# Two-product values at every fourth tile, and a transform family at both ends of one tile

## Chip, cores and metric

The kernel runs on one core of a Trainium2 chip. The metric is the time on the device in microseconds, as the median of several executions. The core has the engines TensorE (PE in the profile; its weight loads are PEld), VectorE (DVE), ScalarE (ACT), GpSimd (POOL) and SyncE (SP), which work side by side and wait for each other through semaphores.

## The reference

```python
X = np.fft.fft(x, axis=1)            # x: 8 x 3008 x 256, float32
X = np.fft.fft(X, axis=2)
y = X.real.reshape(24064, 256)
gate = np.maximum(y @ w_gate, 0.0)   # w_gate, w_val: 256 x 1536
val = y @ w_val
out = gate * val @ w_out             # w_out: 1536 x 256
```

## The kernel before, in words

**Transform.** The transform along the channels is worked into the weights (WA for cosines, WB for sines, WM = -2 WB). The one along the sequence is done by products with tables of cosines and sines, one batch ahead of its use. Its input is folded by symmetry on GpSimd first (`fold_steps`), spread over the tiles by a budget of microseconds per tile (`fold_us`, `run_fold`). The result of a batch is a cosine part U and a sine part V. A batch needs four families of six products (L589): three for one half (`par` 1), copied from PSUM to `es` by ScalarE (L598, `turned_out`), then three for the other half added in the same bank, copied by ScalarE (L601) and combined with `es` by two operations on VectorE (L603, `sums`). From batch 1 on both halves use the one bank d.

**Tiles.** From batch 1 on each batch has three thirds of columns (512, 512 and 481) and in each third 12 tiles of 128 hidden units, so 36 tiles, here numbered 0 to 35. A tile gives 2n columns of the hidden array `h`, since U and V give a value at a row and at its mirror image: the gate and the value are each taken for cosine plus sine and for cosine minus sine.

**A normal tile** ("n") has five products on TensorE:
- L1021 (`sine_part`, bank g) and L1028 (`cosine_part`, bank p). ScalarE puts a bias row into p beforehand (`seed`, L1016) and copies g (L1024). VectorE combines them to the one gate sum (`both`, L1032), GpSimd to the other (L1033).
- L876 and L877 (`value`, bank v): the value at the row. VectorE multiplies it with the rectified gate into the first half of `h` (`relu_mult(.., 0)`, L912).
- L882 (`mirror`): adds to v to make the value at the mirror row, one tile later. VectorE then writes the second half of `h` (`second`, L912 again).

**A two-product tile** (`st["short"]`) has no L882. Its value is built in bank d, of which there is one: ScalarE puts a bias row there two tiles ahead (`seed_value`, L1049), L1053 adds the cosine product one tile ahead (`value_cosine`), ScalarE copies the double of it (L1054), and L1058 adds the sine product (`value_sine`, weights WV, which L1247 makes in batch 2). The mirror value is the doubled copy less bank d. In batches 2 to 5 VectorE subtracts it into bank d itself (L1065, `own`), and `second` is on VectorE; in batches 6 and 7 it subtracts into the copy (L1067) and GpSimd multiplies (L1068). Before, these are tiles 14, 20, 26 and 32 in batches 2 to 5, 14, 18, 22, 26, 30 and 34 in batch 6, and nine in batch 7.

**A joined tile** ("j") makes up for the extra operation on VectorE: its sine product (L1043) is added to p one tile later, ScalarE makes both copies (L1039, L1044), GpSimd subtracts (L1045), and it has no L1032. Before, these are tiles 17, 23, 29 and 35 in batches 2 to 5, three behind each two-product tile.

**The order.** `slot` issues one tile's work for four tiles at once: `cur` (value, first half), `mid` (one ahead: L1043, L1053), `nxt` (two ahead: sine, cosine, `both`) and `pending` (one back: mirror, second half). All engines execute their own instructions in the order of this program. Between the products of a tile stand output products of the third before (L784, 12 per 128 rows, two such groups to a bank o; an eviction by ScalarE, L797, then DMAs by SyncE, L809): `outs` of them per slot, 8 or 7 by `per_tile`, plus or minus some by tile. `out(5)` has issued five eighths of them by the time of L1028; the rest stands at the slot's end. `outs` loses two in the slot ahead of a two-product tile, gains one in its own and in the one behind it, gains two where `nxt` is joined and loses two where `mid` is. `DFT_EVEN` says how many of a batch's 24 transform products follow each slot.

Of the kernel before, what the change touches and what calls it, by code (L numbers as in the profile page):

```python
# [15 lines left out]
ALU = mybir.AluOpType  # L16
# [18 lines left out]
def kernel(  # L35
# [808 lines left out]

    DFT_0 = (0, 0, 0, 0, 0, 3, 0, 0, 4, 3, 3, 0), (0, 0, 0, 0, 0) + (1,) * 7, (3, 3, 3, 3, 3, 3, 0, 0, 0, 0, 0, 0)

    DFT_EVEN = (3, 3, 0) * 4 + (0,) * 24
    DFT_1 = (3, 0, 3, 0, 0, 0) * 4 + (0, 1, 0, 1, 1) + (0,) * 7
    todo_out, todo_dft, todo_fold = [], [], []
    credit, paired = 0, False  # L850
# [2 lines left out]
    def run(todo, n):  # L853
        for _ in range(min(n, len(todo))):
            todo.pop(0)()
        if not paired:
            flush()

    def run_one(todo):
        if todo:  # L860
            todo.pop(0)()
# [53 lines left out]
    def second(st):  # L915
        (relu_mult if "s" in st else mult)(st, 1)
        if st["n"] == 481:
            keep_rest(st)
# [77 lines left out]
    SHORT = (2, 6, 10)  # L996

    def new_tiles():
        for b in range(1, B):
            for blk, block in enumerate(thirds):  # L1000
                for fi in range(NF):
                    st = tile_of(block, fi, uv[b])
                    st["b"] = b
                    mixed = 1 < b < 6 and blk > 0
                    st["kind"] = "o" if (b, blk, fi) == (1, 0, 6) else "j" if mixed and fi in (5, 11) else "n"
                    st["own"] = mixed
                    st["short"] = mixed and fi in (2, 8) or (b, blk) in ((6, 1), (6, 2), (7, 0), (7, 1)) and fi in SHORT or (b, blk) == (7, 2) and fi in (2, 5, 8)
                    st["lead"] = (b, blk, fi) == (1, 0, 0)
                    yield st

# [49 lines left out]
    def value_second(st):  # L1060
        n = st["n"]
        a = st["a"][:, 0:n]
        if st["own"]:
            v = st["v"][:, 0:n]
            nc.vector.tensor_tensor(v, a, v, op=ALU.subtract)  # L1065
            return
        nc.vector.tensor_tensor(a, a, st["v"][:, 0:n], op=ALU.subtract)  # L1067
        nc.gpsimd.tensor_tensor(half_h(st, 1), st["s"][2][:, 0:n], a, op=ALU.mult)  # L1068
        if n == 481:
            keep_rest(st)  # L1070

    def slot(cur, mid, nxt, after, outs, fold_us):

        joined, ready = (st is not None and st["kind"] == "j" for st in (nxt, mid))
        outs += 2 * joined - 2 * ready
        outs += cur["short"] + (pending is not None and pending.get("short", False)) - 2 * (mid is not None and mid["short"])
        stop = len(todo_out)

        def out(part):
            run(todo_out, len(todo_out) - stop + outs * part // 8)  # L1080
        old = nxt is not None and nxt["kind"] == "o"
        new = nxt is not None and nxt["kind"] == "n"
        early = cur["b"] > 1
        if early:
            run_one(turned_out)
            run_one(sums)
            if not todo_dft:
                run_one(sums)
        if old:
            gate(nxt)  # L1090
        lead = cur["lead"]
        out(4 if lead else 0)
        if new and mid["kind"] != "o":
            sine_part(nxt)
        out(4 if lead or nxt is None else 5)
        if new and mid["kind"] == "o":
            sine_part(nxt)
        if ready:
            add_sine(mid)
        if (new or joined) and not lead:  # L1100
            cosine_part(nxt)
        if joined:
            copy_cosine(nxt)
        if not lead:
            seed(after)
        if pending is not None and pending.get("short"):
            value_second(pending)
        elif pending is not None:
            mirror(pending["v"], pending, 1)
            second(pending)  # L1110
        if cur["short"]:
            value_sine(cur)
        else:
            value(cur)
        if mid is not None and mid["short"]:
            value_cosine(mid)
        if cur["kind"] == "o":
            mult(cur, 0, cur["first"])
        else:
            relu_mult(cur, 0)  # L1120
        if pending is not None and pending.get("short") and pending["own"]:
            second(pending)
        if lead:
            out(5)
            cosine_part(nxt)
            seed(after)
        if new:
            both(nxt)
        if old:
            nxt["first"] = nxt["r"]  # L1130
            mirror(nxt["g"], nxt, 0)
            relu(nxt)
        if cur["short"] and not cur["own"]:
            sm = cur["s"][2][:, 0:cur["n"]]
            nc.scalar.activation(sm, sm, ACTF.Relu)
        if nxt is not None and nxt["short"]:
            seed_value(nxt)
        run_fold(fold_us)
        if turned_out and not early:
            run_one(turned_out)  # L1140
        elif not joined:
            run_one(evict)
        if not early:
            run_one(sums)
        out(8)
        return cur
# [4 lines left out]
    for b in range(B):  # L1151
# [4 lines left out]
        for blk, block in enumerate(blocks):  # L1156
# [44 lines left out]
            if (b, blk) == (0, 0):  # L1201
                for fi in range(NF):
                    st = tile_of(block, fi, (U, V, CB))
                    add_h(st, hs)
                    if fi == 8:
                        todo_out = out_steps(b, block, hs, True)
                    pending = first_tile(st, more.get((0, fi), ()), 6)
                mirror(pending["g"], pending, 0)
                relu(pending)
            elif not paired:  # L1210
                for fi in range(NF):
                    st = tile_of(block, fi, (U, V, CB))
                    add_h(st, hs)
                    tag = {(3, 8): "g", (3, 9): "d", (3, 10): "g", (3, 11): "d"}.get((blk, fi), "p")
                    last = []
                    if (blk, fi) == (3, 11):
                        last = [lambda: (sine_part(ahead[1]), cosine_part(ahead[1]), both(ahead[1]), seed(ahead[2]))]
                    if (blk, fi) == (3, 9):
                        ahead = [next(tiles) for _ in range(3)]
                        more[(3, 9)] += [lambda: seed(ahead[0])]  # L1220
                        more[(3, 10)] += [lambda: seed(ahead[1])]
                        more[(3, 11)] += [lambda: (sine_part(ahead[0]), cosine_part(ahead[0]), both(ahead[0]))]
                    if (blk, fi) == (1, 8):
                        run(todo_out, len(todo_out))
                        todo_out = out_steps(b, block, hs, True)
                    st["widen"] = (blk, fi) in ((3, 6), (3, 7))
                    pending = single_tile(st, 3 if blk == 1 else per_tile // 2, more_b.get((blk, fi), ()), last, tag)
                    run(todo_dft, DFT_0[blk - 1][fi])
            else:
                for fi in range(NF):  # L1230
                    at = NF * blk + fi
                    cur = ahead.pop(0)
                    add_h(cur, hs)
                    ahead.append(next(tiles, None))
                    if b < 2:
                        outs = per_tile + ((-2, 0, -2, 2, 2, 0)[fi % 6] if per_tile == 7 else 0)
                    else:
                        outs = per_tile + (0 if blk or b == B - 1 else (-1, -1, 2)[fi % 3])
                    if (b, blk) == (B - 1, 2) and fi > 8:
                        outs = (10, 9, 19)[fi - 9]  # L1240
                        if fi == 9:
                            rest = out_steps(b, block, hs)
                            early, rest = rest[:10] + rest[12:16], rest[10:12] + rest[16:]
                            todo_out += early
                    if (b, at) in ((2, 5), (2, 9), (2, 13)):
                        f = slice(128 * (at - 5), 128 * (at - 1))
                        nc.scalar.mul(WV[:, f], WM[1][:, f], -0.5)  # L1247
                    if (b, at) == (2, 0):
                        nc.sync.dma_start(out=WB[0][0:1, :], in_=WM[0][0:1, :])
                    pending = slot(cur, *ahead, outs, .72 if b < 2 else (.76, .54, .54)[blk])  # L1250
                    for step in more_1.get(at, ()) if b == 1 else ():
                        step()
                    run(todo_dft, DFT_1[at] if b == 1 else DFT_EVEN[at])
            if b or blk > 1:
                run(todo_out, len(todo_out))
            if blk == len(blocks) - 1 or (b, blk) == (0, 1):
# [41 lines left out]
```

## Time and profile before

| | |
|---|---|
| median of 3 runs | 621.99 us (621.98 to 622.07) |
| the profiled execution | 621.7 us, of it 619.6 us span |
| granted TensorE clock | 1.00 |
| instructions with a busy time | 4032 on TensorE, 978 on VectorE, 911 on ScalarE, 493 on GpSimd |

The span reaches from the first to the last instruction that the trace has. A row of the timeline has the start, the duration, the engine, the line, the operation, what it writes and reads, and its size; "x2" means two merged in one row, and a bracket at its end the idle time of that engine before it and what ended it. A row of the groups has the count, the busy time, the mean duration in ns of one, and the idle time before them. Matmuls overlap: their durations are latencies, and what a product costs the engine is the distance from its start to the next.

### The profile page before, as it was taken

To read this page: it belongs to the slowest core of one execution; us is meant where nothing else is said; L and a number is where in the kernel's file an instruction comes from. 1 tells how busy PE (TensorE), PEld (TensorE's weight loads), DVE (VectorE), ACT (ScalarE), POOL (GpSimd) and SP (SyncE) were. 2 spreads that over 40 slices of the span, in tenths; PEclk is the share of its full clock that TensorE was granted. 3 is DMA by queue.
4 is the path that set the end of the run, shared out by engine and by line. 5 is a ranking of instruction groups with operands and counts; after the bars stand their busy time and mean duration, and the time that the engine had idled before them with its cause. 6 is when DMAs were issued, how large, how long until landed. Compare 5 with 4: busy or idle time off the path is not lost.

```text
span 619.6 us, 12415 instructions
## 1 busy us (share of the span) xinstructions
PE 610.7 (99%) x4032; PEld 395.3 (64%) x4076; DVE 549.5 (89%) x978; ACT 485.4 (78%) x911; POOL 520.5 (84%) x493
## 2 busy tenths in 40 slices
PE   8999999999999999999999999999999999999997
PEld 2566666666666666666666666666666666666666
DVE  8886677999899999899999999989999999999991
ACT  7796667776778888778887788777887799999982
POOL 8988992898999989899888988898896588888880
PEclk9999999999999999999999999999999999999999
DMA  9965758735263515524164321621111111211113
GB/s 242 214 199 133 169 175 113 185 75 153 76 152 138 168 52 110 177 76 152 37 159 154 114 94 42 143 70 60 53 44 55 60 44 39 60 52 53 48 47 105
DMA packets 86035, 66.48 MB, mean 107 GB/s; under 512 B 41639, under 2 KB 69063, under 8 KB 85970
## 3 DMA queue, kind: packets, MB, share of 16 engines
q1 hardware_dynamic: 81384, 60.02, 35.5%
q0 software_dynamic: 3984, 4.92, 4.0%
q8 instruction: 32, 0.52, 0.4%
q10 hardware_dynamic: 602, 0.75, 0.3%
q14 instruction: 33, 0.27, 0.2%
HBM read 41.89 MB, written 34.17 MB: 123 GB/s over the span
## 4 chain that ended last, share of the span: by engine, by line
PE 95%; DVE 1%; POOL 1%; issue 1%; DMA 1%; ACT 0%; DVEq 0%; POOLq 0%; ACTq 0%
PE o L784 39%; PE v L877 10%; PE v L882 9%; PE p L1028 8%; PE g L1021 8%; PE v L876 7%; PE d L589 4%; PE p L882 1%; PE d L1058 1%; PE d L1053 1%; PE p L876 1%; PE p L877 1%; DMA XG<-in_x_dram,gidx 1%; PE o L427 1%; PE p L1043 1%
## 5 line engine op out<-in xcount | busy, mean ns | idle before, releaser
L1033 POOL TENSOR_TENSOR r<-r 128x512 f32<-128x512 f32 (+1 forms) x235 | 293.4, 1254 | 75.0 <-DVE r L1032 73.8
L784 PE MATMUL o<-wo,h 128*128 128x256 bf16 x2172 | 328.6, 272 | 0.0
L912 DVE SCALAR_TENSOR_TENSOR h<-r,v 128x512 bf16<-128x512 f32 (+1 forms) x440 | 281.0, 674 | 32.9 <-PE v L882 24.6
L784 PEld LDWEIGHTS <-h 128*128 128x128 bf16 x2220 | 216.7, 98 | 109.8 <-issue 0.9
L1016 ACT ACTIVATE p<-CB,b 128x512 f32<-128x512 bf16 (+1 forms) x251 | 172.4, 687 | 32.1 <-DVE r L1032 28.6
L1024 ACT COPY r<-g 128x512 f32<-128x512 f32 (+1 forms) x235 | 135.9, 578 | 30.8 <-PE g L1021 27.6
L1032 DVE SCALAR_TENSOR_TENSOR r<-r,p 128x512 f32<-128x512 f32 (+1 forms) x235 | 157.4, 670 | 0.8 <-ACT r L1024 0.8
L877 PE MATMUL v<-V,WB 128*128 128x512 bf16 (+3 forms) x265 | 97.0, 366 | 2.2
L1028 PE MATMUL p<-U,WA 128*128 128x512 bf16 (+1 forms) x251 | 94.1, 375 | 0.0
L1021 PE MATMUL g<-V,WM 128*128 128x512 bf16 (+1 forms) x235 | 88.2, 375 | 0.2
L882 PE MATMUL v<-V,WM 128*128 128x512 bf16 (+1 forms) x221 | 82.8, 375 | 0.2 <-DVE h L912 0.2
L876 PE MATMUL v<-U,WA 128*128 128x512 bf16 (+3 forms) x223 | 81.1, 364 | 0.0
L901 DVE TENSOR_TENSOR h<-r,v 128x376 bf16<-128x376 f32 (+2 forms) x90 | 46.1, 546 | 16.4 <-PE v L882 11.3
L797 ACT COPY os<-o 128x512 f32<-128x512 f32 x92 | 52.5, 570 | 2.8 <-PE o L784 2.8
L198 POOL TENSOR_TENSOR XG<-XG,XD 128x510 f32<-128x510 f32 x42 | 52.9, 1271 | 0.9 <-DMA XG<-xr 0.9
L892 ACT ACTIVATE r<-p 128x376 f32<-128x376 f32 (+1 forms) x80 | 38.3, 487 | 18.0 <-PE p L882 8.6
L876 PEld LDWEIGHTS <-WA 128*128 128x128 bf16 x317 | 30.9, 97 | 32.2 <-issue 10.5
L877 PEld LDWEIGHTS <-WB 128*128 128x128 bf16 x317 | 30.9, 97 | 30.1 <-ACT WB L680 0.2
L206 POOL TENSOR_TENSOR AA<-XG 128x510 f32<-128x510 f32 x42 | 45.5, 1094 | 0.0
L912 DVE SCALAR_TENSOR_TENSOR h<-r,d 128x512 bf16<-128x512 f32 (+1 forms) x47 | 31.3, 667 | 0.0
L1028 PEld LDWEIGHTS <-WA 128*128 128x128 bf16 x251 | 24.6, 98 | 3.3 <-issue 0.2
L1021 PEld LDWEIGHTS <-WM 128*128 128x128 bf16 x235 | 23.0, 98 | 5.5 <-issue 0.3
(201 smaller groups left out, 597.3 us busy)
## 6 DMA issues: line engine op xcount, KB each, us to landing
out_dram<-os SPq DMA_DIRECT2D x124, 128.0 KB
xr<-in_x_dram SPq DMA_DIRECT2D x12, 768.0 KB
XG<-xr SPq DMA_DIRECT2D x12, 768.0 KB
XD<-in_x_dram SPq DMA_DIRECT2D x15, 512.0 KB
out_dram<-os SPq DMA_DIRECT2D x35, 112.0 KB
XD<-in_x_dram SPq DMA_DIRECT2D x8, 448.0 KB
CB<-ch SPq DMA_DIRECT2D x7, 376.2 KB
out_dram<-os SPq DMA_DIRECT2D x13, 96.0 KB
```

The lines of the kernel that those rows point to most:

```text
L198: e.tensor_tensor(XG[p, r, t, ::-1, 1:D], XG[p, r, t, ::-1, 1:D], XD[p, r, t, :, D - 1:0:-1], op=ALU.add)
L784: nc.tensor.matmul(st["p"][0:m, q, :], lhsT=lhs(f), rhs=wo[:, f, :], start=(f == 0 and not (early and q)), stop=(f == NF - 1), skip_group_ ...
L876: nc.tensor.matmul(bank[:, 0:st["n"]], lhsT=WA[i][:, st["f"]], rhs=st["us"], start=True, stop=False)
L877: nc.tensor.matmul(bank[:, 0:st["n"]], lhsT=WB[i][:, st["f"]], rhs=st["vs"], start=False, stop=True)
L882: nc.tensor.matmul(bank[:, 0:st["n"]], lhsT=W[i][:, st["f"]], rhs=v, start=False, stop=True, skip_group_check=True)
L912: nc.vector.scalar_tensor_tensor(half_h(st, sign), in0=st["s"][1 + sign][:, 0:n], scalar=0.0, in1=st["v"][:, 0:n], op0=ALU.max, op1=ALU.mult)
L1016: nc.scalar.activation(st["p"][:, 0:st["n"]], st["c"], ACTF.Copy, scale=b2[:, st["fi"]:st["fi"] + 1])
L1021: nc.tensor.matmul(st["g"][:, 0:n], lhsT=WM[0][:, st["f"]], rhs=st["vs"], start=True, stop=True)
L1024: nc.scalar.copy(q[:, 0:n], st["g"][:, 0:n])
L1028: nc.tensor.matmul(st["p"][:, 0:n], lhsT=WA[0][:, st["f"]], rhs=st["us"], start=False, stop=True, skip_group_check=True)
L1032: nc.vector.scalar_tensor_tensor(sp[:, 0:n], in0=q[:, 0:n], scalar=-0.5, in1=st["p"][:, 0:n], op0=ALU.mult, op1=ALU.add)
L1033: nc.gpsimd.tensor_tensor(sm[:, 0:n], sp[:, 0:n], q[:, 0:n], op=ALU.add)
```

## The change

- Two-product tiles come at every fourth tile from tile 10 on (10, 14, 18, 22, 26, 30, 34) in batches 2 to 6; batch 7 keeps its own.
- A joined tile follows two behind each one of batches 2 to 5 (12, 16, ..., 32, and tile 0 of the next batch).
- The subtraction in bank d (`own_second`) goes to the end of the tile's own slot, behind its first half; the second half comes first in the next slot.
- A family's two halves stand at the two ends of one slot, in tiles 0, 2, 4 and 6: three products at the slot's head, ahead of everything else on TensorE, the copy to `es` right behind them on ScalarE, and three products at the slot's end. Before, three products followed each of tiles 0, 1, 3, 4, 6, 7, 9 and 10.
- The output products of the first third are spread anew (-4 and +3 by turns, then +1), as are the fold budgets (.78, .52, .50 us for .76, .54, .54) and the making of WV (ahead of tiles 1, 3 and 5 of batch 2, not 5, 9 and 13).

Lines behind L996 move by three to six: L1021, L1028, L1053, L1058 and L1065 of before are L1024, L1031, L1056, L1061 and L1073 of after.

```diff
--- before.py
+++ after.py
@@ -844,7 +844,7 @@
 
     DFT_0 = (0, 0, 0, 0, 0, 3, 0, 0, 4, 3, 3, 0), (0, 0, 0, 0, 0) + (1,) * 7, (3, 3, 3, 3, 3, 3, 0, 0, 0, 0, 0, 0)
 
-    DFT_EVEN = (3, 3, 0) * 4 + (0,) * 24
+    DFT_EVEN = (6, 0) * 4 + (0,) * 28
     DFT_1 = (3, 0, 3, 0, 0, 0) * 4 + (0, 1, 0, 1, 1) + (0,) * 7
     todo_out, todo_dft, todo_fold = [], [], []
     credit, paired = 0, False
@@ -996,15 +996,18 @@
     SHORT = (2, 6, 10)
 
     def new_tiles():
+        own = [False] * 2
         for b in range(1, B):
             for blk, block in enumerate(thirds):
                 for fi in range(NF):
                     st = tile_of(block, fi, uv[b])
                     st["b"] = b
-                    mixed = 1 < b < 6 and blk > 0
-                    st["kind"] = "o" if (b, blk, fi) == (1, 0, 6) else "j" if mixed and fi in (5, 11) else "n"
-                    st["own"] = mixed
-                    st["short"] = mixed and fi in (2, 8) or (b, blk) in ((6, 1), (6, 2), (7, 0), (7, 1)) and fi in SHORT or (b, blk) == (7, 2) and fi in (2, 5, 8)
+                    at = NF * blk + fi
+                    two_ = at % 4 == 2 and at > 9
+                    st["kind"] = "o" if (b, blk, fi) == (1, 0, 6) else "j" if own[0] else "n"
+                    st["own"] = two_ and 1 < b < 6
+                    own = own[1:] + [st["own"]]
+                    st["short"] = st["own"] or b == 6 and two_ or (b, blk) in ((7, 0), (7, 1)) and fi in SHORT or (b, blk) == (7, 2) and fi in (2, 5, 8)
                     st["lead"] = (b, blk, fi) == (1, 0, 0)
                     yield st
 
@@ -1060,16 +1063,16 @@
     def value_second(st):
         n = st["n"]
         a = st["a"][:, 0:n]
-        if st["own"]:
-            v = st["v"][:, 0:n]
-            nc.vector.tensor_tensor(v, a, v, op=ALU.subtract)
-            return
         nc.vector.tensor_tensor(a, a, st["v"][:, 0:n], op=ALU.subtract)
         nc.gpsimd.tensor_tensor(half_h(st, 1), st["s"][2][:, 0:n], a, op=ALU.mult)
         if n == 481:
             keep_rest(st)
 
-    def slot(cur, mid, nxt, after, outs, fold_us):
+    def own_second(st):
+        v = st["v"][:, 0:st["n"]]
+        nc.vector.tensor_tensor(v, st["a"][:, 0:st["n"]], v, op=ALU.subtract)
+
+    def slot(cur, mid, nxt, after, outs, fold_us, turned):
 
         joined, ready = (st is not None and st["kind"] == "j" for st in (nxt, mid))
         outs += 2 * joined - 2 * ready
@@ -1084,8 +1087,9 @@
         if early:
             run_one(turned_out)
             run_one(sums)
-            if not todo_dft:
-                run_one(sums)
+            run_one(sums)
+            run(todo_dft, turned // 2)
+            run_one(turned_out)
         if old:
             gate(nxt)
         lead = cur["lead"]
@@ -1103,7 +1107,9 @@
             copy_cosine(nxt)
         if not lead:
             seed(after)
-        if pending is not None and pending.get("short"):
+        if pending is not None and pending.get("own"):
+            second(pending)
+        elif pending is not None and pending.get("short"):
             value_second(pending)
         elif pending is not None:
             mirror(pending["v"], pending, 1)
@@ -1118,8 +1124,8 @@
             mult(cur, 0, cur["first"])
         else:
             relu_mult(cur, 0)
-        if pending is not None and pending.get("short") and pending["own"]:
-            second(pending)
+        if cur["own"]:
+            own_second(cur)
         if lead:
             out(5)
             cosine_part(nxt)
@@ -1235,22 +1241,22 @@
                     if b < 2:
                         outs = per_tile + ((-2, 0, -2, 2, 2, 0)[fi % 6] if per_tile == 7 else 0)
                     else:
-                        outs = per_tile + (0 if blk or b == B - 1 else (-1, -1, 2)[fi % 3])
+                        outs = per_tile + (0 if blk or b == B - 1 else (-4, 3, -4, 3, -4, 3, -4, 3, 1, 1, 1, 1)[fi])
                     if (b, blk) == (B - 1, 2) and fi > 8:
                         outs = (10, 9, 19)[fi - 9]
                         if fi == 9:
                             rest = out_steps(b, block, hs)
                             early, rest = rest[:10] + rest[12:16], rest[10:12] + rest[16:]
                             todo_out += early
-                    if (b, at) in ((2, 5), (2, 9), (2, 13)):
-                        f = slice(128 * (at - 5), 128 * (at - 1))
+                    if (b, at) in ((2, 1), (2, 3), (2, 5)):
+                        f = slice(256 * (at - 1), 256 * (at + 1))
                         nc.scalar.mul(WV[:, f], WM[1][:, f], -0.5)
                     if (b, at) == (2, 0):
                         nc.sync.dma_start(out=WB[0][0:1, :], in_=WM[0][0:1, :])
-                    pending = slot(cur, *ahead, outs, .72 if b < 2 else (.76, .54, .54)[blk])
+                    pending = slot(cur, *ahead, outs, .72 if b < 2 else (.78, .52, .5)[blk], DFT_EVEN[at])
                     for step in more_1.get(at, ()) if b == 1 else ():
                         step()
-                    run(todo_dft, DFT_1[at] if b == 1 else DFT_EVEN[at])
+                    run(todo_dft, DFT_1[at] if b == 1 else DFT_EVEN[at] // 2)
             if b or blk > 1:
                 run(todo_out, len(todo_out))
             if blk == len(blocks) - 1 or (b, blk) == (0, 1):
```

## The prediction

> **What bounds the kernel now.** I read the head of the page first, then the list of TensorE groups, then the timeline around single tiles.
>
> ```profile
> span 619.6 us, 12415 instructions
> ...
> PE 610.7 (99%) x4032; PEld 395.3 (64%) x4076; DVE 549.5 (89%) x978; ACT 485.4 (78%) x911; POOL 520.5 (84%) x493
> ...
> PE 95%; DVE 1%; POOL 1%; issue 1%; DMA 1%; ACT 0%; DVEq 0%; POOLq 0%; ACTq 0%
> ```
>
> TensorE is busy 99% of the span and holds 95% of the chain that ended last. So a product taken away is worth its own interval, unless a wait grows in its place. The page's idle columns hide such waits, because the modelled ends of matmuls overlap the next start. They show when starts are compared, in the timeline of batch 3 around tiles 13 and 14 (tile 14 is a two-product tile):
>
> ```profile
> 276.68 0.38 PE L1028 MATMUL p<-U,WA 128*128 128x512 bf16 x1
> ...
> 276.90 0.38 PE L882 MATMUL v<-V,WM 128*128 128x512 bf16 x1
> ...
> 277.39 1.28 DVE L912 SCALAR_TENSOR_TENSOR h<-r,v 128x512 bf16<-128x512 f32 x2 [0.18 <-PE v L882]
> ...
> 278.09 0.49 PE L784 MATMUL o<-wo,h 128*128 128x256 bf16 x3
> ...
> 278.42 0.38 PE L1028 MATMUL p<-U,WA 128*128 128x512 bf16 x1
> ...
> 278.59 0.68 DVE L1032 SCALAR_TENSOR_TENSOR r<-r,p 128x512 f32<-128x512 f32 x1
> 278.72 0.38 PE L882 MATMUL v<-V,WM 128*128 128x512 bf16 x1
> 278.73 0.10 PEld L876 LDWEIGHTS <-WA 128*128 128x128 bf16 x1 [0.21 <-issue]
> 278.94 0.38 PE L876 MATMUL v<-U,WA 128*128 128x512 bf16 x1
> ...
> 279.15 0.38 PE L877 MATMUL v<-V,WB 128*128 128x512 bf16 x1
> ```
>
> A 512-column product takes 0.216 us from start to start (278.72, 278.94, 279.15), an output product (L784, 256 columns) 0.109 (three from 278.09 to 278.42). At 276.68 the mirror product L882 follows L1028 after 0.22, as it should. At 278.42 it follows after 0.30: TensorE stood still for 0.09 us. What it waited for is VectorE: the mirror at 276.90 releases the second half at 277.39 (0.49 later), then comes the first half of the next tile, together 1.28 (two of 0.68, so 0.60 from start to start), end 278.67, and 0.05 later the next mirror. This **loop** takes 0.49 + 0.60 + 0.68 + 0.05 = 1.82 us. TensorE's work between these two mirrors is five products and six output products, 5 x 0.216 + 6 x 0.109 = 1.73, hence 0.09 lost. A normal tile has eight output products, 1.95, and loses nothing. The slot ahead of every two-product tile has two output products fewer (`- 2 * mid["short"]`), so each such tile brings one such stop. The same in 481 columns (tile 26 of batch 3):
>
> ```profile
> 301.48 0.37 PE L1028 MATMUL p<-U,WA 128*128 128x481 bf16 x1
> ...
> 301.79 0.36 PE L882 MATMUL v<-V,WM 128*128 128x481 bf16 x1
> ...
> 301.99 0.36 PE L876 MATMUL v<-U,WA 128*128 128x481 bf16 x1
> ...
> 302.20 0.36 PE L877 MATMUL v<-V,WB 128*128 128x481 bf16 x1
> ...
> 302.26 1.23 DVE L912 SCALAR_TENSOR_TENSOR h<-r,v 128x481 bf16<-128x481 f32 x2
> ...
> 303.40 0.65 DVE L1032 SCALAR_TENSOR_TENSOR r<-r,p 128x481 f32<-128x481 f32 x1
> ...
> 457.47 0.37 PE L1028 MATMUL p<-U,WA 128*128 128x481 bf16 x1
> 457.75 0.36 PE L882 MATMUL v<-V,WM 128*128 128x481 bf16 x1
> ```
>
> Here a product takes 0.203, the stop is 0.11 at tile 26, where 512 turns into 481, and 0.08 later in the third (457.47 to 457.75). VectorE's step is 0.57 (302.26 + 1.23 - 0.65 = 302.84 to 303.40 is 0.56; the pair has 1.23 - 0.65 = 0.58), and mirror to second half 0.47 (301.79 to 302.26).
>
> **The change, part by part.**
>
> *Products removed.* Two-product tiles are now 31:
>
> ```profile
> L1058 PE MATMUL d<-V,kvec 128*128 128x512 bf16 x17 | 6.4, 379 | 0.0
> ...
> L1058 PE MATMUL d<-V,kvec 128*128 128x481 bf16 x14 | 5.1, 367 | 0.0
> ```
>
> By the new rule they are 7 instead of 4 in each of batches 2 to 5 (tiles 10, 14, 18, 22, 26, 30, 34), 7 instead of 6 in batch 6, and 9 as before in batch 7: 44. The built order has 13 matmuls fewer. Nine have 512 columns and four 481: 9 x 0.216 + 4 x 0.203 = **-2.75**. Output products only move between slots and keep their number.
>
> *A, the stop ahead of a two-product tile.* The product count of that slot is unchanged (five and six outputs), so the loop stops it as now. Batches 2 to 5 gain one stop of 0.09 and one of 0.08 each: 0.68. Tile 10 lies in the first third: in batches 3 and 5 the slots there have nine outputs and the stretch is 1.95, no stop; in 2, 4 and 6 they have eight, 1.73, one of 0.09 each: 0.27. Sum **+0.95**.
>
> *B, the moved subtraction.* VectorE's queue was subtract, first half of the next tile, second half, all in the slot after the two-product tile k. Now it is first half of k, subtract, second half of k, first half of k+1. The number of operations is the same (a joined tile needs no L1032, and it now comes two tiles behind, in the very slot that has the subtraction), but the second half reads what the operation just before it wrote. The trace of before has no such pair in its steady part; the nearest are in the setup:
>
> ```profile
> 13.70 1.22 DVE L461 TENSOR_TENSOR AA<-XG,XD 121x1020 f32<-121x1020 f32 x1 [0.39 <-issue]
> 15.03 0.17 DVE L462 TENSOR_TENSOR AA<-XG,XD 121x8 f32<-121x8 f32 x1
> 15.23 0.43 DVE L441 TENSOR_TENSOR F<-AA 121x258 bf16<-121x258 f32 x1
> ...
> L1065 DVE TENSOR_TENSOR d<-r,d 128x512 f32<-128x512 f32 x8 | 5.5, 689 | 0.0
> L1065 DVE TENSOR_TENSOR d<-r,d 128x481 f32<-128x481 f32 x8 | 5.2, 656 | 0.0
> ```
>
> L462 needs L461 and another wait: it starts 0.11 after L461's end (14.92). L441 needs L462 alone: 0.03. Independent operations start 0.08 before the end (0.68 - 0.60). The second half waits for two things, the subtraction and GpSimd's sum, so I take 0.10; the ends are 0.03 and, if nothing is held up, -0.08. Behind it stand the first half of k+1 and through it the mirror of k+1. From the mirror of k-1 to that of k+1: 0.49 + 0.60 + 0.60 + 0.69 + 0.10 + 0.60 + 0.68 + 0.05 = 3.81. TensorE between them: nine products and 17 outputs (5 of slot k, 7 of k+1, 5 of k+2), 9 x 0.216 + 17 x 0.109 = 3.79. So about 0.02 is lost at 10 places (tiles 14, 18 of four batches, tile 10 of batches 2 and 4): 0.20. At tile 22 five of the nine products already have 481 columns: 3.73, 0.08 x 4 = 0.32. In 481 columns the chain is 0.47 + 0.58 + 0.57 + 0.66 + 0.10 + 0.57 + 0.65 + 0.05 = 3.65 against 9 x 0.203 + 17 x 0.109 = 3.68: nothing. Sum **+0.52**.
>
> *C, the transform at the front of a batch.* The first three products of a family now stand at the head of tile 0. They write bank d, of which there is one, and tile 34 of batches 2 to 5 still holds it: the release is its second half, the fourth operation of the chain B. From the mirror of 33: 0.47 + 0.58 + 0.57 + 0.66 + 0.10 + 0.65 + 0.05 = 3.08. TensorE has until then three products of 512, four of 481 and 12 outputs: 0.65 + 0.81 + 1.31 = 2.77. Everything behind stands in TensorE's queue: 0.31 at the start of batches 3, 4, 5 and 6: **+1.23**. Before, the last two-product tile was 32 and the transform stood at the end of tile 0, so the bank was long free.
>
> *D, the transform's slots.* Tile 1's stretch ahead of batches 2, 4 and 6 was short too:
>
> ```profile
> 177.35 0.38 PE L1028 MATMUL p<-U,WA 128*128 128x512 bf16 x1
> ...
> 177.63 0.36 PE L882 MATMUL v<-V,WM 128*128 128x481 bf16 x1
> ```
>
> 0.28 where 0.22 is due: 0.06 lost. With three transform products in it that stretch grows over the loop: **-0.17**. In the other slots of the transform the stretches, counted the same way, become 2.1 to 2.5. VectorE's two sums (0.34 each, below, 0.26 apart by the overlap of 0.08) lie between two halves there; the worst stretch, 2.1, starts with them done, since the mirror ahead of it stands 2.4 behind the one before. So they cost nothing; uncovered they would cost 0.5 per family.
>
> *ScalarE, GpSimd, SyncE.* ScalarE gets 39 more instructions of about 0.6, 23 us on 485, 82% of the span; GpSimd one more. Where a two-product tile needs ScalarE now:
>
> ```profile
> 280.06 0.59 ACT L1054 ACTIVATE r<-d 128x512 f32<-128x512 f32 x1
> ...
> 281.10 0.38 PE L1058 MATMUL d<-V,kvec 128*128 128x512 bf16 x1
> ...
> L603 DVE SCALAR_TENSOR_TENSOR V<-es,d 128x188 bf16<-128x188 f32 x24 | 8.2, 342 | 0.0
> ...
> L797 ACT COPY os<-o 128x512 f32<-128x512 f32 x92 | 52.5, 570 | 2.8 <-PE o L784 2.8
> ...
> L1247 ACT ACTIVATE kvec<-WM 128x512 bf16<-128x512 bf16 x3 | 1.9, 621 | 0.0
> ```
>
> The doubled first product is out at 280.65, the next write to the bank at 281.10, 0.45 later. The new slot loses a sine product and gains one output ahead of it, 0.11 less; where an eviction of 0.57 (L797) falls into the slot before, some 0.2 stays. I cost this at nothing. The three copies L1247 move into the transform's slots of batch 2, where the stretches are longest; uncovered, 0.6 each. The fold budgets (.78, .52, .50) put GpSimd's steps within one slot of where they stand. The two row DMAs (L1189, L1192) leave SyncE's queue four slots earlier, when the sums that they wait for are done, and are read a batch later: nothing.
>
> *Sum.* -2.75 + 0.95 + 0.52 + 1.23 - 0.17 = **-0.2 us**. The profiled execution took 621.7 (span 619.6 and 2.1 around it), 0.3 below the median of the runs, 621.99. I expect 621.5 for a profiled run and 621.8 for the median.
>
> **Rivals.** *VectorE's handover costs nothing.* If the second half starts 0.60 after the subtraction as after any other operation, B's chain is 3.62 and never late, C's is 2.88 and costs 0.11 x 4: -2.75 + 0.95 + 0.44 - 0.17 = -1.5, 620.5. Against it stands the gap of 0.11 behind L461. The Trainium skill, "VectorE: DVE Perf Modes", section "The DRAIN you can't avoid", says that the next operation does not start until the pipe empties and that a semaphore between chained operations costs nothing extra; by that rule this rival would hold, and the rows of L461 and L462 speak against it. With 0.03 for the gap B falls to 0.08 and C to 0.94: 621.0, within the forecast's own band.
>
> *ScalarE becomes late (the other side).* Place: the doubling copy of tile k, or the seed two tiles on, in the slots where an eviction precedes it. The point is the 0.2 that I left there. If it is 0.1 late at all 28 tiles of batches 2 to 5, +2.8: 624.6; at every third, +0.9: 622.7. For it: two more instructions per tile pair in the same slots. Against: ScalarE stays 18% idle.
>
> *The handover is dearer in PSUM.* Both sides of it lie in bank d, those of L461 do not. With 0.1 more, 18 chains of 512 columns or at a batch's start cost 1.8 and eight of 481, less their 0.03, 0.5: 624.1. Against: once it runs, an operation on d takes as long as one on v (0.68):
>
> ```profile
> L912 DVE SCALAR_TENSOR_TENSOR h<-r,d 128x512 bf16<-128x512 f32 x25 | 17.0, 680 | 0.0
> ```
>
>
> That no products are saved is excluded by the built order.
>
> **How the numbers follow.** Forecast (621.0 to 622.8): 0.62. Handover free, 620.5: 0.16. ScalarE late: 0.14, of it 0.04 under 623.2. Handover dearer: 0.08. A measurement tells about 0.2%, 1.24 us, from no change, so the forecast is "same"; the first rival is faster, the others slower but for 0.04 that stays within. Faster 0.16, same 0.66, slower 0.18. The range takes in the free handover and stops below the dear ones: 620.3 to 623.4.
>
> **What would show it.** In the profile after, L1061 x44 in place of L1058 x31. Starts of L1031 and L882 0.30 apart ahead of each two-product tile (A). At the start of batches 3 to 6 a hole of about 0.3 ahead of the first L589, ended by VectorE (C). The second half about 0.10 behind the end of the subtraction L1073 (B). L1057 ending at least 0.1 ahead of L1061. The forecast is wrong if C is missing, if the gap behind L1073 is not near 0.1, or if TensorE waits for ScalarE in these slots.

## The result, and the profile after

| | before | after |
|---|---|---|
| median | 622.18 us (621.98 to 622.52, 6 runs) | 627.68 us (626.77 to 629.59, 6 runs) |
| profiled execution | 621.7, span 619.6 | 628.44, span 626.7 |

The ratio is 1.0092, interval 1.0081 to 1.0103: the change costs 5.5 us. 621.8 was forecast, with 620.3 to 623.4 as the range. Three of the six executions after lie at 626.77 to 626.93 with a granted clock of 1.000; three, the profiled one among them, at 628.44 to 629.59 with 0.996 to 0.997.

The head of the page of after: span, busy times, the shares of the chain that ended last, and the group of the output products.

```profile
span 626.7 us, 12448 instructions
...
PE 612.3 (98%) x4019; PEld 394.1 (63%) x4063; DVE 551.8 (88%) x978; ACT 509.1 (81%) x950; POOL 521.6 (83%) x494
...
PE 91%; DMA 3%; DVE 3%; issue 2%; POOL 1%; ACT 1%; DVEq 0%; ACTq 0%; POOLq 0%
...
L784 PE MATMUL o<-wo,h 128*128 128x256 bf16 x2172 | 327.5, 273 | 2.0 <-ACT os L797 2.0
```

TensorE has its 13 products fewer (4032 to 4019), yet the span is 7.1 longer and TensorE's share of the chain falls from 95 to 91%. What took it stands in the waits of TensorE (engine, what it writes, line, what it waited for: us in total, times, longest):

```profile
PE d L568 <- DMA WB<-WM: 2.5, 1, 2.5
PE o L784 <- ACT os L797: 2.0, 3, 0.7
...
PE d L589 <- DVE h L912: 0.5, 1, 0.5
```

The first two rows are new, and no step of the prediction has them; the third is the front of a batch, part C.

**First missed wait: a transfer.** L568 (`widen`) is a small product at the end of one transform half. It reads WB[0], and a row of WB[0] is brought by a DMA that SyncE issues before tile 0 of batch 2 (L1249 before, L1255 after). In the timeline of SyncE and in the chain of after:

```profile
181.64 5.02 SPq L1255 DMA_DIRECT2D WB<-WM  x1
```

```profile
181.64 13.98 DMA WB<-WM
```

It lands 14 us after its issue, at 195.62. In before the same transfer is issued at 181.83 and its semaphore has its last count at 195.60. The timeline of TensorE in before has L568 5.2 us behind that, at the end of tile 10:

```profile
200.30 0.65 PE L589 MATMUL d<-tabC,F 128*128 128x377 bf16 x3
200.78 0.22 PE L568 MATMUL d<-WB,WA 128*128 128x135 bf16 x1
```

The change puts that half at the end of tile 6, so L568 is due 7.7 us earlier (at 195.67 - 2.55 = 193.12). In the timeline of TensorE after:

```profile
195.67 0.22 PE L568 MATMUL d<-WB,WA 128*128 128x135 bf16 x1 [2.55 <-DMA WB<-WM]
195.72 0.38 PE L1024 MATMUL g<-V,WM 128*128 128x512 bf16 x1
195.94 1.22 PE L784 MATMUL o<-wo,h 128*128 128x256 bf16 x6
196.96 0.63 PE L1031 MATMUL p<-U,WA 128*128 128x512 bf16 x1
197.38 0.64 PE L882 MATMUL v<-V,WM 128*128 128x512 bf16 x1
197.81 0.64 PE L876 MATMUL v<-U,WA 128*128 128x512 bf16 x1
```

TensorE stands 2.55 us by this row (2.71 counted from start to start). Behind it a product takes 0.43 from start to start (197.38, 197.81) instead of 0.216. The table of stretches says why (us, then the busy times of PE, PEld, DVE, ACT, POOL with counts, then the granted clock, the DMA share and GB/s):

```profile
191.00:195.60 4.60, 2.12 (x13) 1.07 (x11) 2.98 (x5) 1.57 (x3) 4.56 (x4) 1.00 0.40 147
195.67:199.85 4.18, 4.18 (x18) 2.32 (x18) 2.24 (x5) 2.07 (x4) 0.27 (x1) 0.59 0.47 130
199.85:204.00 4.15, 4.10 (x29) 2.67 (x29) 3.31 (x6) 3.42 (x6) 3.50 (x3) 1.00 0.23 72
```

After the stop the clock is 0.59 for 4.18 us, which loses 0.41 x 4.18 = 1.7 us more. The three executions with the lower mean clock lie 1.6 (this one), 2.0 and 2.7 us above the mean of the other three; only this one has a trace.

**Second missed wait: an eviction.** At tile 12 of batch 2, TensorE and then ScalarE in the timelines of after:

```profile
206.93 0.49 PE L784 MATMUL o<-wo,h 128*128 128x256 bf16 x3
207.25 0.38 PE L1024 MATMUL g<-V,WM 128*128 128x512 bf16 x1
208.35 0.71 PE L784 MATMUL o<-wo,h 128*128 128x256 bf16 x5 [0.72 <-ACT os L797]
```

```profile
206.48 0.59 ACT L1047 COPY r<-p 128x512 f32<-128x512 f32 x1
207.10 0.69 ACT L1019 ACTIVATE p<-CB,b 128x512 f32<-128x512 bf16 x1
207.73 0.58 ACT L797 COPY os<-o 128x512 f32<-128x512 f32 x1
```

L784 should follow L1024 after 0.22, at 207.47; it starts 0.88 later, when the eviction of its bank ends (208.31). In batches 2, 4 and 6 the first third has 84 output products: three banks of 24 and one of 12. The last bank is full 12 products after the third, so the third must be evicted at once. `slot` evicts at most once, at its end, and not at all when `nxt` is joined. Tile 10's slot is such a one (tile 12 is joined), so the eviction comes last on ScalarE in slot 11, just as the next third wants the bank. In batch 6, where tile 12 is not joined, the slot ahead of the two-product tile 10 has two products fewer, and by the kernel's own counts the third bank has 71 of its 72 products at tile 10's eviction point. It costs 0.88, 0.88 and 0.73, together 2.50.

**What was foreseen.** A two-product tile, tile 14 of batch 3, in the timeline of TensorE after, and its doubling copy on ScalarE:

```profile
283.58 0.38 PE L1031 MATMUL p<-U,WA 128*128 128x512 bf16 x1
283.89 0.38 PE L882 MATMUL v<-V,WM 128*128 128x512 bf16 x1
...
285.73 0.38 PE L1031 MATMUL p<-U,WA 128*128 128x512 bf16 x1
285.95 0.38 PE L882 MATMUL v<-V,WM 128*128 128x512 bf16 x1
286.16 0.38 PE L1061 MATMUL d<-V,kvec 128*128 128x512 bf16 x1
```

```profile
285.37 0.59 ACT L1057 ACTIVATE r<-d 128x512 f32<-128x512 f32 x1
```

L1031 to L882 takes 0.31 ahead of the tile, a stop of 0.09, and 0.22 in it. The copy ends at 285.96, 0.20 before L1061. The front of batch 3, TensorE and VectorE, and the same operations on VectorE at the front of batch 6:

```profile
253.32 0.49 PE L784 MATMUL o<-wo,h 128*128 128x256 bf16 x3
253.96 0.64 PE L589 MATMUL d<-tabS,G 128*128 128x376 bf16 x3
```

```profile
252.49 0.66 DVE L1073 TENSOR_TENSOR d<-r,d 128x481 f32<-128x481 f32 x1
253.25 0.66 DVE L912 SCALAR_TENSOR_TENSOR h<-r,d 128x481 bf16<-128x481 f32 x1
```

```profile
471.01 0.66 DVE L1073 TENSOR_TENSOR d<-r,d 128x481 f32<-128x481 f32 x1
472.13 0.66 DVE L912 SCALAR_TENSOR_TENSOR h<-r,d 128x481 bf16<-128x481 f32 x1 [0.46 <-DVE d L1073]
```

The second half starts 0.10 behind the end of the subtraction (253.15 to 253.25), as it does at 27 of the 28 places. The three output products take 0.33, so L589 was due at 253.65 and comes 0.31 late. At batch 6 the same handover takes 0.46, and the front waits 0.67 from start to start (0.51 in its row of the waits).

Counted from start to start, TensorE's stops in the two profiled executions stand like this:

| term | forecast | measured |
|---|---|---|
| 13 products removed | -2.75 | -2.75 (count and intervals as before) |
| stops ahead of L882 (A, B, D) | +1.30 | +1.27 |
| front of batches 3 to 6 (C) | +1.23 | +1.61 (0.31 three times, 0.67) |
| L568 waits for the transfer | none | +2.71 |
| lower clock behind it | none | +1.68 |
| L784 waits for the eviction | none | +2.50 |
| sum | -0.2 | +7.0 (the two spans differ by 7.1, the two times by 6.74) |

### The profile page after: what moved, and what is told of

It reads as the page before. It is cut to its first block, busy times and chain, and to the rows that moved or that the text cites. A ratio compares the mean times of both kernels' runs of the same rounds, so it can differ in the third digit from the quotient of the medians.

```text
span 626.7 us, 12448 instructions
## 1 busy us (share of the span) xinstructions
PE 612.3 (98%) x4019; PEld 394.1 (63%) x4063; DVE 551.8 (88%) x978; ACT 509.1 (81%) x950; POOL 521.6 (83%) x494
## 4 chain that ended last, share of the span: by engine, by line
PE 91%; DMA 3%; DVE 3%; issue 2%; POOL 1%; ACT 1%; DVEq 0%; ACTq 0%; POOLq 0%
PE o L784 37%; PE v L882 9%; PE v L877 9%; PE p L1031 8%; PE g L1024 7%; PE v L876 6%; PE d L589 4%; DMA WB<-WM 2%; PE d L1056 1%; PE d L1061 1%; DVE h L912 1%; PE p L882 1%; PE p L876 1%; PE p L877 1%; DMA XG<-in_x_dram,gidx 1%
## 5 line engine op out<-in xcount | busy, mean ns | idle before, releaser
L1036 POOL TENSOR_TENSOR r<-r 128x512 f32<-128x512 f32 (+1 forms) x223 | 278.1, 1252 | 76.5 <-DVE r L1035 76.0
L784 PE MATMUL o<-wo,h 128*128 128x256 bf16 x2172 | 327.5, 273 | 2.0 <-ACT os L797 2.0
L912 DVE SCALAR_TENSOR_TENSOR h<-r,v 128x512 bf16<-128x512 f32 (+1 forms) x414 | 266.0, 675 | 31.2 <-PE v L882 26.1
L784 PEld LDWEIGHTS <-h 128*128 128x128 bf16 x2220 | 216.8, 98 | 110.5 <-issue 4.3
L1035 DVE SCALAR_TENSOR_TENSOR r<-r,p 128x512 f32<-128x512 f32 (+1 forms) x223 | 149.6, 671 | 0.8 <-ACT r L1027 0.8
L1027 ACT COPY r<-g 128x512 f32<-128x512 f32 (+1 forms) x223 | 128.8, 577 | 16.5 <-PE g L1024 11.3
L877 PE MATMUL v<-V,WB 128*128 128x512 bf16 (+3 forms) x252 | 92.4, 367 | 2.2
L1031 PE MATMUL p<-U,WA 128*128 128x512 bf16 (+1 forms) x251 | 94.4, 376 | 0.0
L1024 PE MATMUL g<-V,WM 128*128 128x512 bf16 (+1 forms) x223 | 83.8, 376 | 0.2
L882 PE MATMUL v<-V,WM 128*128 128x512 bf16 (+1 forms) x208 | 78.2, 376 | 0.2 <-DVE h L912 0.2
L876 PE MATMUL v<-U,WA 128*128 128x512 bf16 (+3 forms) x210 | 76.5, 364 | 0.0
L797 ACT COPY os<-o 128x512 f32<-128x512 f32 x92 | 52.7, 573 | 2.8 <-PE o L784 2.8
L912 DVE SCALAR_TENSOR_TENSOR h<-r,d 128x512 bf16<-128x512 f32 (+1 forms) x72 | 48.3, 671 | 3.3 <-DVE d L1073 0.5
L876 PEld LDWEIGHTS <-WA 128*128 128x128 bf16 x304 | 29.6, 97 | 33.8 <-issue 13.3
L1048 POOL TENSOR_TENSOR r<-r 128x512 f32<-128x512 f32 (+1 forms) x28 | 34.9, 1247 | 5.0 <-ACT r L1047 4.4
L598 ACT COPY es<-d 128x377 f32<-128x377 f32 (+1 forms) x30 | 14.2, 474 | 19.6 <-PE d L589 18.7
```

The costliest lines, as they stand in the source:

```text
L784: nc.tensor.matmul(st["p"][0:m, q, :], lhsT=lhs(f), rhs=wo[:, f, :], start=(f == 0 and not (early and q)), stop=(f == NF - 1), skip_group_ ...
L876: nc.tensor.matmul(bank[:, 0:st["n"]], lhsT=WA[i][:, st["f"]], rhs=st["us"], start=True, stop=False)
L877: nc.tensor.matmul(bank[:, 0:st["n"]], lhsT=WB[i][:, st["f"]], rhs=st["vs"], start=False, stop=True)
L882: nc.tensor.matmul(bank[:, 0:st["n"]], lhsT=W[i][:, st["f"]], rhs=v, start=False, stop=True, skip_group_check=True)
L912: nc.vector.scalar_tensor_tensor(half_h(st, sign), in0=st["s"][1 + sign][:, 0:n], scalar=0.0, in1=st["v"][:, 0:n], op0=ALU.max, op1=ALU.mult)
L1024: nc.tensor.matmul(st["g"][:, 0:n], lhsT=WM[0][:, st["f"]], rhs=st["vs"], start=True, stop=True)
```

## The experiments

Theory: the sum is right but for two waits that it lacks, the transfer (with the clock that falls behind it) and the eviction. Rivals: that a wait taken away only makes room for another, and that more is missing than these two.

**The transfer alone.** L568 writes columns of bank d past those that the family uses, so it can multiply any table; WB[1] has no row that a DMA brings.

```diff
-        nc.tensor.matmul(p[:, n:512], lhsT=WA[0][:, 0:128], rhs=WB[0][:, 0:512 - n], ...
+        nc.tensor.matmul(p[:, n:512], lhsT=WA[0][:, 0:128], rhs=WB[1][:, 0:512 - n], ...
```

> The changed kernel, where the filling product L568 reads row block WB[1] instead of WB[0]; only unused columns of bank d differ. My theory: the changed kernel loses about 2.7 us at this product in batch 2, because it now stands at tile 6 and the transfer of one row into WB[0], issued at the front of that batch, lands later; where the granted clock falls behind it another 1.7. So this kernel takes about 624.3, all its executions close together, and its clock is 1.00. Rival: the extra instructions on ScalarE are the limit, the wait moves elsewhere and the time stays at 626 or above.

Measured: 624.46 us (624.12 to 624.72), ratio 1.0037 [1.0023, 1.0051], clock 0.999 to 1.000 in all five executions. The wait for the DMA is gone from the table of waits and the stop of 0.88 at tile 12 is left. The transfer costs 627.68 - 624.46 = 3.2 us in the median, 2.4 against the executions of after at full clock.

**The eviction alone.** One more eviction at the head of tile 11.

```diff
         if early:
+            if cur["at"] == 11:
+                run_one(evict)
             run_one(turned_out)
```

> The changed kernel with one more eviction call at the head of tile 11's slot. My theory: at tile 12 of batches 2, 4 and 6 TensorE waits 0.88, 0.88 and 0.73 for the eviction of bank o, because the last output group there has 12 products instead of 24 and the eviction behind it comes a slot late. So 2.5 us less: 624.4 in executions with a clock of 1.00, about 626 in those with a drop. Rival: ScalarE is too loaded there, what goes ahead of the copies delays them, and less than half of it is won.

Measured: 626.09 us, ratio 1.0059 [1.0045, 1.0073]. One execution at clock 1.000 has 624.76, four at 0.997 have 625.78 to 626.52. L797 is gone from TensorE's waits, the DMA is still there:

```profile
PE d L568 <- DMA WB<-WM: 2.3, 1, 2.3
```

At full clock, by this one execution, the eviction is worth 626.86 (the mean of after's three) - 624.76 = 2.1, of the 2.5 that stood in the trace. The moved eviction puts the seed behind it late: in batches 2 and 4 L1031 waits 0.12 each, by the trace of the next run.

**Both.** The two edits together.

> After with the two missed waits taken away together: L568 reads WB[1] instead of the row that the DMA brings, and the eviction of the first third's last full bank comes at the head of tile 11. The transform's front half stays where the change put it, so the prediction's own terms are left: products -2.75, stops ahead of two-product tiles +0.95, chain through the bank +0.52, front of batches 3 to 6 +1.23 and 0.36 more as measured at batch 6, tile 1 -0.17, and 0.2 for the moved eviction's own waits. Theory (the sum was right but for the two waits that it lacked): 622.2 + 0.3 = 622.5 (622.0 to 623.0), clock 1.00 in every execution. Rival (more is missing from the sum than these two): 623.4 or more.

Measured: 622.01 us (621.70 to 622.51, 11 runs) beside 622.14 before, ratio 0.9998 [0.9989, 1.0007], clock 0.999 to 1.000. That is close to the 621.8 of the forecast: with the two waits out, no third one of their size is missing. That it is this close is in part luck. The trace has the front 0.36 above its forecast and two waits of 0.12 from the moved eviction, which is why 622.5 was expected here, and the measured time is 0.5 lower, at the lower edge of the range. In medians the span is 0.2 longer than that of before (620.2 and 620.0), and the time outside the span, which the prediction carried over from before as 2.1, is 1.8 here; what makes it shorter stays open. TensorE's waits, of the changed part only the front of the batches is left:

```profile
PE o L326 <- DVE warm L317: 1.2, 1, 1.2
PE d L589 <- DVE h L912: 0.8, 3, 0.5
```

**Which part of the change brings the transfer's wait.** The kernel before with the transform part alone: its tiles stay, the family's halves go to the two ends of a slot.

```diff
-    DFT_EVEN = (3, 3, 0) * 4 + (0,) * 24
+    DFT_EVEN = (6, 0) * 4 + (0,) * 28
...
+            run(todo_dft, turned // 2)
+            run_one(turned_out)
...
-                        ... (0 if blk or b == B - 1 else (-1, -1, 2)[fi % 3])
+                        ... (0 if blk or b == B - 1 else (-4, 3, -4, 3, -4, 3, -4, 3, 1, 1, 1, 1)[fi])
```

> The kernel before with one part of the change alone: both halves of a family at the two ends of tiles 0, 2, 4, 6, and the new spread of the first third's output products; two-product tiles as before. My theory: the row transfer into WB[0] is waited for by this part alone, so +2.5 us (+1.7 more where the clock drops), -0.2 for the stops of 0.06 at tile 1 that go, nothing else: 624.5 with a clock of 1.00, 626.2 with a drop. Rival: part of the loss at the transform comes from the two-product tiles' load on ScalarE; then this kernel is below 623.5.

Measured: 625.87 us, ratio 1.0060 [1.0046, 1.0074]; 623.92 in the one execution at full clock, 625.22 to 627.03 at 0.997. So the transform part brings the wait by itself, without one new two-product tile:

```profile
PE d L568 <- DMA WB<-WM: 2.1, 1, 2.1
```

Its table of waits has no row of L784 behind L797: the new spread alone does not make the eviction late, it takes the new places of the tiles as well.

**The front of the batches.** The family's first half goes behind L1031 of its slot, and its copy behind the seed, so that bank d is free by then. This run has the rest of after as it is:

```diff
-            run(todo_dft, turned // 2)
-            run_one(turned_out)
...
             cosine_part(nxt)
+        if early:
+            run(todo_dft, turned // 2)
...
             seed(after)
+        if early and turned:
+            run_one(turned_out)
```

> The changed kernel with the first half of a family behind L1031 instead of at the slot's head. My theory: the holes of 0.31 ahead of the first L589 of batches 3 to 6 (0.67 at batch 6 in the profile) go, since 0.8 us of other work now covers them: 1.2 to 1.6 less, 625.5 in executions with a clock of 1.00. Rival: the copy to es comes later and the second half waits for it: no gain.

> The changed kernel with all three edits. My theory: what is left is the forecast's sum without its part C, -2.75 + 0.95 + 0.52 - 0.17 = -1.45 against the kernel before, 620.7. Rival (load on ScalarE or VectorE is the limit): 624 or more, with new waits of TensorE for ScalarE.

Measured: 633.85 us (633.48 to 634.76) for this edit alone, ratio 1.0192 [1.0178, 1.0206]; 631.31 (630.91 to 631.51) with the two edits above beside it, 1.0147. The rival of the first run was right (it said no gain; it is a loss of 6.2 us against after), and the expectation of the second fell with it. TensorE's waits and a timeline of this kernel, first TensorE, then ScalarE, at the end of the first tile of batch 3:

```profile
PE d L589 <- ACT es L598: 6.8, 20, 0.6
```

```profile
253.81 0.27 PE L784 MATMUL o<-wo,h 128*128 128x256 bf16 x1
254.36 0.64 PE L589 MATMUL d<-tabS,G 128*128 128x376 bf16 x3 [0.27 <-ACT es L598]
```

```profile
253.84 0.46 ACT L598 COPY es<-d 128x376 f32<-128x376 f32 x1
```

These rows are from the first of the two runs. The copy that empties bank d ends at 254.30, when the second half is already due: with the first half and its copy later in the slot, too little of it is left for ScalarE. The stop at the front went (ahead of batches 4 and 6 one of 0.29 at L1031 came in its place), and 20 others came, one for each of the four families of five batches; 6.8 is their idle time in the table, from start to start they are some 10. In the first run L568 does not wait for the transfer any more, since these stops bring it to its place later.

**The front once more.** After with both edits above and the first half a little earlier, ahead of L1031, its copy right behind it:

```diff
-            run(todo_dft, turned // 2)
-            run_one(turned_out)
...
         out(5)
+        if early and turned:
+            run(todo_dft, turned // 2)
+            run_one(turned_out)
         if ready:
             add_sine(mid)
```

> As e4_three, but the first half of a family stands between the slot's first output products and its cosine product L1031, and the copy to es comes right behind it on ScalarE, ahead of the seed. My theory: in e3 and e4 the copy to es stood behind the seed, which waits for VectorE, and the second half waited for it 20 times, 6.8 us; here the copy is out in time, and the 0.33 to 0.43 ahead of the products still cover the 0.31 that bank d is late. So the forecast without C holds, plus 0.1 twice for the moved eviction: 621.0. Rival: the second halves still wait, 624 or more.

Measured: 620.71 us (620.23 to 621.12, 9 runs), ratio 0.9978 [0.9968, 0.9988]. Against the run with both edits this is 622.01 - 620.71 = 1.3 us, most of the cost of the front. It was forecast at 1.23 and takes 1.61 in the trace of after; here a stop of 0.34 is left of it, at batch 6. The place in batch 3 in the timelines of TensorE and ScalarE:

```profile
248.66 0.64 PE L589 MATMUL d<-tabS,G 128*128 128x376 bf16 x3
...
250.22 0.65 PE L589 MATMUL d<-tabS,G 128*128 128x376 bf16 x3
```

```profile
249.34 0.47 ACT L598 COPY es<-d 128x376 f32<-128x376 f32 x1
```

The copy ends at 249.81, 0.41 before the second half.

**The stop ahead of a two-product tile, by itself.** In the kernel before the slot ahead of such a tile issues seven eighths of its output products by the time of L1028, in place of five. No product is added or taken away; the stretch between two mirrors gets longer, as the loop of 1.82 us asks.

```diff
-        out(4 if lead or nxt is None else 5)
+        out(4 if lead or nxt is None else 7 if early and mid is not None and mid["short"] else 5)
```

> The kernel before, where the slot ahead of a two-product tile issues five of its six output products ahead of the mirror instead of three (seven eighths instead of five); nothing is added or taken away. My theory (part A of the prediction): each of 31 stops of 0.06 to 0.11 goes, about 2.8 us in all: 619.4. Rival: VectorE itself is the limit there, so the stop moves to the next mirror and at most 0.5 us is won.

Measured: 619.88 us (619.55 to 620.12), ratio 0.9963 [0.9950, 0.9976]: 2.2 us won of the 2.8 expected. In the trace the stops ahead of L882 from batch 2 on fall from 3.2 us in all to 0.6, so the loop that the prediction read off the timeline of before is what stops TensorE there.

**All together.** After with the two edits, the earlier first half and this split.

> As e9_before_cosine, with the split of e7: five of six output products ahead of the mirror in the slot ahead of a two-product tile. My theory: 44 stops of part A, about 3.8 us, go; left of the forecast's sum are -2.75, B +0.5 and D -0.17 against the kernel before without its own 31 stops (2.8): 617.1. Rival: without those stops ScalarE or VectorE becomes the limit: 619 or more.

Measured: 617.49 us (617.25 to 617.76), ratio 0.9925 [0.9912, 0.9938]. It beats both kernels, before by 4.6 us and after by 10.2:

```profile
span 615.6 us, 12443 instructions
```

## Why the prediction was wrong

The forecast of no change failed at two of its steps, both of which cost something that moves at nothing.

*D, the transform's slots.* The step weighed the moved products against VectorE ("the worst stretch, 2.1, starts with them done ... So they cost nothing"). It counted products and sums and left out L568, the product behind the three, and so did not ask what L568 reads. Its operand comes by a transfer that is 14 us under way, and the half moved to a place ahead of the end of that transfer. Both rows were in the trace of before (L568 at 200.78, the DMA issued at 181.83), they only had no idle time on them. The run that takes away this wait and nothing else brought back 3.2 us in the median, 2.4 at full clock.

*Products removed.* "Output products only move between slots and keep their number" is true and not enough. With them moves the moment at which a bank is full, and the eviction has one place per slot and none in the slot two ahead of a joined tile. TensorE waited 2.50 us for it, and the run with one more eviction won 2.1. In before the third bank is full in tile 10's slot, by the kernel's counts just ahead of its eviction point, and the first joined tile is 17. The prediction checked evictions for the doubling copy only, and there it was right: L1057 keeps 0.20.

The rest held, point by point. A: in batches 2 to 6 0.09 ahead of the two-product tiles of 512 columns, and 0.11 (tile 26) or 0.08 ahead of those of 481, as forecast; the run with the moved split shows the loop as its cause. B: 0.02 at tiles 14 and 18 and 0.085 at tile 22 (0.08 forecast), with a handover of 0.10; the 0.02 at tile 10 of two batches does not show. C: 0.31 three times of the four; the fourth, 0.67, was mis-sized by 0.36, by a hole on VectorE that stays unexplained (below). D without L568: the stop of 0.06 at tile 1 is gone.

Of the rivals, the free handover is out: 0.104 in 27 of 28 places. The Trainium skill, "VectorE: DVE Perf Modes", section "The DRAIN you can't avoid", says of a chain of copies that the semaphore between them costs nothing extra; here the second half starts 0.10 behind the end of the subtraction (252.49 + 0.66 = 253.15 to 253.25), where the operation behind it, L912 at 253.82, starts 0.09 ahead of the second half's end (253.25 + 0.66 = 253.91). The dearer handover is out by the same number. "ScalarE becomes late" named the right engine at the wrong place: the doubling copies and seeds keep up, and the eviction that is late is late by its place in the program, not by ScalarE's load of 81%: the run with one more eviction has no such wait. So of the signs that the prediction named for its being wrong, a wait of TensorE for ScalarE came, though at tile 12 and not at the doubling copy. None of the rivals had the transfer, so the range could not reach the result.

## What to carry to other kernels

When a step moves earlier, list the operands of every instruction in it, the small ones too, and find when each of them lands: a transfer that ends ahead of its reader had no idle time in this profile until the reader moved ahead of its end. When work is only redistributed, follow the buffers it fills and not its count: look for the slot in which the buffer is emptied, and for the shortest group. And the bounds that were read as loops between engines, start to start, came out here within 0.05 us at all places but one (the front of batch 6, 0.36 off), so a short sum of such loops that misses by several microseconds lacks a term.

## What the runs showed of the hardware

- A stop of TensorE of 2.3 to 2.7 us from start to start (2.1 to 2.55 in the idle column) is followed in the three traces that have it by some 4 us at a granted clock of 0.59, with products 0.43 apart. The mean clock is 0.996 to 0.997 in three of six executions of after and in four of five and five of six of the two other kernels with this wait (the eviction alone, the transform part alone). These executions take 1.4 to 2.3 us more, in the mean of each kernel, than its executions at full clock, of which no trace is there. Without that stop no execution of a kernel here fell under 0.999. The Trainium skill, "TensorE: Matmul & The Clock Gate", section "Why this matters for your kernels", asks for no idle gaps over about 3 us. Here a shorter one was enough, though not each time.
- A transfer of one row of 3 KB took 14 us from issue to landing, with the output's transfers under way beside it. In the trace its semaphore has ten of its sixteen counts after 6 us and the last six after 13 to 14; which of them stand for data does not show. The Trainium skill, "DMA: Bandwidth & Descriptors", section "Why a DMA increments its semaphore by 16 and not by 1", says that only the full sixteen mean that all data has landed; the wait of L568 agrees, since it ends 0.05 behind the last count (195.62 to 195.67).
- VectorE's second half at the front of batch 6 starts 0.46 behind the subtraction, where 27 others start 0.10 behind, in after and in the seven experiments with its tiles. What it waits for by the trace is done 0.45 ahead of it (the subtraction at 471.67, GpSimd's sum at 471.44), and it lies at the same place of VectorE's order each time (the 753rd of its 978 operations). What makes it stays open; no run here was aimed at it.
